# Weights converted by shifted words and fetched behind the first chunk; the two MLP products one and three steps behind attention

## The chip, the cores and the metric

The kernel runs on one NeuronCore of a Trainium2 chip. The metric is device time in microseconds, launch to end, of the compiled program. A core has a matrix engine (PE, which also has a queue of its own for loading weights into the array, PEld), VectorE (DVE), ScalarE (ACT), GpSimd (POOL) and SyncE (SP), which here only issues DMAs. Each engine takes its instructions in program order and waits on semaphores of the others.

## The reference

The input is a gated linear attention over 4 sequences of 768 tokens, 8 heads of 48, followed by an MLP with a SoLU activation and a layer norm on the resulting 3072 tokens of 384.

```python
for t in range(S):
    state = alpha[:, :, t, :, None] * state + np.einsum('bhd,bhe->bhde', k[:, :, t], v[:, :, t])
    y[:, :, t] = np.einsum('bhd,bhde->bhe', q[:, :, t], state)
...
h = x @ w_in                      # x: 3072 x 384, w_in: 384 x 1024
e = np.exp(h - h_max)
sm = e / (np.sum(e, axis=-1, keepdims=True) + 1e-09)
solu = h * sm
ln = (solu - mu) / np.sqrt(var + 1e-06) * g_ln
return (ln @ w_out).astype(np.float32)   # w_out: 1024 x 384
```

The attention inputs are float32. The weights `w_in` and `w_out` arrive as float64 and must be made float32 on the chip.

## The kernel before

The tokens are cut into 24 chunks of 128 (6 positions of each of 4 sequences; chunk n is sequence n mod 4). A main loop runs over steps n. In a step the attention of chunk n is done in matrix form, and two parts run ahead or behind it: the transposes and running products of chunk n+1 are prepared, and the MLP of chunk m = n − 3 is done, both its products in one step (`LAG = 3`, L53).

The attention of a chunk: `load` (L104) fetches alpha, q, k and v with four DMAs on SP; `prep_aq` and `prep_k` transpose them on PE (`tp`, L118) and copy them on ACT (`aT`, `qT`, `kT`, L119); `prep_scan` makes the running products with two scans on DVE (`hT` L132, `qF` L142) and a maximum over alpha (`amax`, L146); `prep_q` and `prep_k` multiply on POOL (L153, L160); `scores` (L181) makes two tiles `a` on PE, masked into `sT` on DVE (L186); `keys_back` transposes k (`tp_k`, L194); `read_out` makes `y` (L204 from the state, from a sequence's second chunk on, and L210 from the scores); `next_state` makes `kv` (L224); `x_T` transposes the result (`tp_x`, L240) into `xT`.

The MLP of a chunk: `up` makes `h` with two halves of 24 matmuls (L256; counted with the weights in two passes), then `e` = Exp(h) on ACT (L261), `u` = h·e on DVE (L262), and the square of `u` on ACT (L263). `partial` adds up eight blocks of e on POOL and of u squared on DVE (L270, L274). `down` multiplies `u` by `w_out` into `o` (L281) and adds two column sums by a matmul with ones (L286). `finish` turns the sums into the norm's scale and stores 128 rows.

The weights: before the loop three chunks are loaded; `weights` (L336) then fetches a piece of raw 64-bit words into one of 2 buffers and converts it with six DVE instructions (L349, L351, L354, L355, L356, L359), one on ACT (L350) and a multiplication on POOL (L362). It masks the mantissa's upper bits, clamps the exponent to what float32 holds, and puts sign, exponent and fraction together. `weights_in` does two of the six pieces of `w_in` in each of the steps 0 to 2; `weights_out` does the eight of `w_out` in steps 1 to 3 and scales each by the gain (L372). In step 3 `centre` (L382) makes the mean over the rows of `w_out` with eight matmuls (L386) and subtracts it with eight instructions, four on DVE and four on POOL (L391). Only then can a `down` start.

A scheduler puts the instructions of each engine in order, starting from the order of the code; it moves independent work forward. What an engine finds in its queue is fixed when the program is built. At the end the kernel checks its own assumptions (`ok`, L443 to L459); if one fails, a general path runs.

## Time and profile before

| what | value |
|---|---|
| time, median of 3 runs | 507.04 us (505.81 to 508.24) |
| profiled execution, its own time | 506.91 us |
| span of its profile | 504.0 us |
| mean granted PE clock | 0.924 |
| DMA | 30.63 MB, mean 61 GB/s |
| SP waits for conversion buffers (L344 on DVE) | 24.6 + 21.0 + 9.2 us |

A profile's page lists the busy time of each engine, the chain of work that ended last, and groups of instructions by source line. A line of a group reads: line, engine, operation, output<-inputs, shapes, count, then busy microseconds and the mean nanoseconds of one, then the idle time of the engine just before and what ended it. The granted clock is the share of full speed that PE was given; at 0.50 a matmul takes twice as long. PE's busy time is modelled, so a busy PE may be a slow one.

### The profile page before, as it was taken

How to read it: one execution, taken by the hardware profiler on the slowest of the kernel's cores; microseconds unless marked ns; L12 is line 12 of the kernel's file. 1: busy time of each engine (PE TensorE's matmuls, PEld its weight loads, DVE VectorE, ACT ScalarE, POOL GpSimd, SP SyncE). 2: the span in 40 equal slices, each digit the busy share in tenths (PEclk: the TensorE clock that was granted, in tenths of full speed). 3: DMA queues.
4: the chain of work that ended last, by engine and by line, in shares of the span. 5: the costliest groups of instructions: out<-in, count | busy, mean ns of one | idle time of the engine just before them, and what ended most of it. 6: DMA issues, size and time to landing. Idle time of an engine off the chain costs nothing.

```text
span 504.0 us, 7993 instructions
## 1 busy us (share of the span) xinstructions
PE 466.2 (93%) x3195; PEld 393.5 (78%) x3195; DVE 284.0 (56%) x555; ACT 155.9 (31%) x288; POOL 187.2 (37%) x201
## 2 busy tenths in 40 slices
PE   4898398698999999999999999999999999999993
PEld 3787276586788988898898898889889888988872
DVE  7488978975544753664565375366455535522332
ACT  4134132331323332342242333234224233423220
POOL 7233624646224423432451342343245234412232
PEclk9558555969999999999999999999999999999998
DMA  9916554400331332222123132222210100000000
GB/s 192 214 43 153 136 135 114 104 20 1 91 70 29 77 64 49 48 64 63 33 64 71 24 78 64 50 45 65 64 33 16 34 9 9 16 17 18 16 17 23
DMA packets 105663, 30.63 MB, mean 61 GB/s; under 512 B 100488, under 2 KB 103824, under 8 KB 105616
## 3 DMA queue, kind: packets, MB, share of 16 engines
q1 hardware_dynamic: 105312, 29.89, 26.1%
q8 instruction: 27, 0.44, 0.4%
q10 hardware_dynamic: 304, 0.14, 0.1%
q14 instruction: 20, 0.16, 0.1%
HBM read 25.30 MB, written 4.72 MB: 60 GB/s over the span
## 4 chain that ended last, share of the span: by engine, by line
PE 87%; DVE 8%; ACT 1%; POOL 1%; DMA 1%; issue 1%; ACTq 0%
PE o L281 25%; PE h L256 24%; PE y L210 9%; PE tp L118 7%; PE a L181 6%; PE kv L224 4%; PE y L204 3%; PE tp_k L194 2%; PE tp_x L240 2%; PE o L286 2%; PE mean L386 1%; DVE qF L142 1%; DVE expo L351 1%; DVE frac L359 1%; DVE bits L349 1%; POOL w_out L362 1%
## 5 line engine op out<-in xcount | busy, mean ns | idle before, releaser
L256 PE MATMUL h<-xT,w_in 128*128 128x128 f32 x1152 | 144.7, 281 | 3.4 <-POOL w_in L362 3.4
L256 PEld LDWEIGHTS h<-xT,w_in 128*128 128x128 f32 x1152 | 138.7, 197 | 6.3 <-POOL w_in L362 4.1
L281 PE MATMUL o<-w_out,u 128*128 128x385 f32 x384 | 129.2, 488 | 2.0 <-POOL w_out L391 2.0
L281 PEld LDWEIGHTS o<-w_out,u 128*128 128x128 f32 x384 | 71.0, 190 | 47.8 <-POOL w_out L391 3.0
L307 POOL TENSOR_TENSOR r<-sums,mhalf 128x1 f32<-128x1 f32 x24 | 13.2, 549 | 127.3 <-DVE sums L303 127.3
L210 PE MATMUL y<-vn,sT 128*128 128x48 f32 x384 | 51.5, 289 | 2.9 <-DVE sT L186 2.9
L210 PEld LDWEIGHTS y<-vn,sT 128*128 128x128 f32 x384 | 50.5, 209 | 4.5 <-DVE sT L186 3.3
L296 DVE COPY sums<-o 128x3 f32<-128x3 f32 x24 | 3.8, 160 | 89.0 <-PE o L286 89.0
L262 DVE TENSOR_TENSOR u<-h,e 128x512 f32<-128x512 f32 x48 | 32.9, 685 | 35.0 <-ACT e L261 32.3
L132 DVE TENSOR_TENSOR_SCAN hT<-aT,unit 128x516 f32<-128x516 f32 x24 | 30.3, 1263 | 38.3 <-ACT aT L119 38.3
L242 ACT COPY xT<-tp_x 128x384 f32<-128x384 f32 x24 | 11.5, 478 | 130.5 <-PE tp_x L240 130.5
L263 ACT ACTIVATE u<-u 128x512 f32<-128x512 f32 x48 | 30.2, 630 | 63.7 <-DVE u L262 55.9
L153 POOL TENSOR_TENSOR qT<-qT,qF 128x512 f32<-128x512 f32 x24 | 30.1, 1254 | 39.7 <-DVE qF L142 39.7
L261 ACT ACTIVATE e<-h 128x512 f32<-128x512 f32 x48 | 28.7, 597 | 42.5 <-PE h L256 42.5
L181 PE MATMUL a<-qT,kT 48*128 48x128 f32 x384 | 37.3, 316 | 4.8 <-POOL qT L153 4.8
L160 POOL TENSOR_TENSOR kT<-kT,hT 128x508 f32<-128x508 f32 x24 | 28.4, 1185 | 35.8 <-ACT kT L119 34.5
L270 POOL TENSOR_TENSOR part_e<-e 128x512 f32<-128x512 f32 x24 | 30.5, 1272 | 25.9 <-ACT e L261 23.8
L274 POOL TENSOR_TENSOR part_e<-part_e 128x256 f32<-128x256 f32 (+1 forms) x48 | 37.8, 787 | 3.8
L181 PEld LDWEIGHTS a<-qT,kT 48*128 48x128 f32 x384 | 30.0, 210 | 11.3 <-POOL qT L153 5.3
L172 POOL TENSOR_TENSOR state<-state,hT 128x384 f32<-128x384 f32 x20 | 16.9, 845 | 49.1 <-DVE hT L132 49.1
L142 DVE TENSOR_TENSOR_SCAN qF<-aT,seed 128x516 f32<-128x516 f32 x24 | 32.1, 1336 | 0.8
L186 DVE TENSOR_TENSOR sT<-a,mask 128x512 f32<-128x512 f32 x48 | 31.0, 680 | 0.8 <-PE a L181 0.7
(79 smaller groups left out, 572.2 us busy)
## 6 DMA issues: line engine op xcount, KB each, us to landing
vn<-in_v_dram SPq DMA_DIRECT2D x24, 192.0 KB, 2.7
an<-in_alpha_dram SPq DMA_DIRECT2D x24, 192.0 KB, 3.4
qn<-in_q_dram SPq DMA_DIRECT2D x24, 192.0 KB, 3.5
kn<-in_k_dram SPq DMA_DIRECT2D x24, 192.0 KB, 3.0
out_dram<-o_sb SPq DMA_DIRECT2D x24, 192.0 KB, 2.0
raw<-in_moe_w_in_dram SPq DMA_DIRECT2D x6, 512.0 KB, 3.8
raw<-in_moe_w_out_dram SPq DMA_DIRECT2D x8, 384.0 KB, 3.2
ident<-ident_c ACTq DMA_DIRECT2D x1, 64.0 KB, 2.3
```

What stands on the lines that cost most here:

```text
L118: nc.tensor.transpose(out=tp[:, j], in_=src[:, 2 * j : 2 * j + 2, :], identity=ident)
L132: nc.vector.tensor_tensor_scan(out=h[:, 0 : NP * SW][:, ::-1], data0=a.rearrange("p j s -> p (j s)")[:, ::-1], data1=unit.rearrange("p j s ...
L142: nc.vector.tensor_tensor_scan(out=d["qF"].rearrange("p j s -> p (j s)"), data0=a.rearrange("p j s -> p (j s)"), data1=s.rearrange("p j s ...
L181: nc.tensor.matmul(a[i][:, j], lhsT=d["kT"][heads[i], j], rhs=d["qT"][heads[i], j], start=True, stop=True)
L186: nc.vector.tensor_tensor(out=d["sT"][:, i], in0=a[i], in1=mask[:, None, :].to_broadcast([P, NP, P]), op=ALU.mult)
L210: nc.tensor.matmul(y[:, h, :], lhsT=d["sT"][:, h % 2, h // 2], rhs=d["v"][:, h], start=(c == 0 and h == 0), stop=(h == H - 1), skip_group_ ...
L256: nc.tensor.matmul(h[:, f], lhsT=w_in[:, a, (f0 + f) * P : (f0 + f + 1) * P], rhs=d["xT"][:, a], start=(a == 0), stop=(a == KC - 1),)
L262: nc.vector.tensor_tensor(out=d["u"][:, fs], in0=h, in1=d["e"][:, fs], op=ALU.mult)
L263: nc.scalar.activation(out=d["u2"][:, fs], in_=d["u"][:, fs], func=AF.Square)
L270: eng.tensor_tensor(out=t, in0=d[key][:, 0:HF], in1=d[key][:, HF:FC], op=ALU.add)
L274: eng.tensor_tensor(out=t[:, 0:w], in0=t[:, 0:w], in1=t[:, w : 2 * w], op=ALU.add)
L281: nc.tensor.matmul(o[:, 0 : DM + 1], lhsT=d["u"][:, f], rhs=w_out[:, f], start=(f == 0), stop=(f == FC - 1), skip_group_check=True,)
```

## The change

Conversion. A weight's upper word, shifted left by three and masked, with its two top bits put back, is already the float32 of the same value up to the lowest mantissa bits (`top`): the exponent's three spare bits fall out. The rest comes from the lower word times 2^-52 times the power of two in `top`. So a piece takes three DVE instructions, one on ACT, a multiplication on POOL, and an addition, on DVE for odd pieces and on POOL for even ones. Nothing clamps the exponent any more. Instead all weights are fetched once more from step 6 on, and two ACT instructions a piece (`in_range`) square the upper words, read as floats, and take Exp of −2^24 times that; their sums enter the final check.

Order. One chunk is loaded ahead of the weights instead of three; then come the fetches of all six pieces of `w_in`, then chunk 1, and so on. There are four raw buffers of their own. Three pieces of `w_in` are converted before the loop and three in step 0; `w_out` is fetched and converted in steps 0 to 2. The first product of chunk n − 1 and the second of chunk n − 3 run in step n. `down` makes its two column sums ahead of the product, from tiles of their own (`sum_e`, `sum_u`), which with `u` are kept for three chunks. `partial` does the same additions.

```diff
-    LAG = 3
+    UP, DOWN = 1, 3
...
-    xtp = pool("xtp", LAG + 1)
+    xtp = pool("xtp", UP + 2)
+    hid = pool("hid", DOWN - UP + 1)
+    rawp = pool("rawp", 4)
...
-            d["u"] = work.tile([P, FC, P], FP, name="u")
+            d["u"] = hid.tile([P, FC, P], FP, name="u")
...
             t = work.tile([P, HF, P], FP, name="part_" + key)
+            s = hid.tile([P, P], FP, name="sum_" + key)
             eng.tensor_tensor(out=t, in0=d[key][:, 0:HF], in1=d[key][:, HF:FC], op=ALU.add)
-            w = HF
+            w = HF // 2
             while w > 1:
+                eng.tensor_tensor(out=t[:, 0:w], in0=t[:, 0:w], in1=t[:, w : 2 * w], op=ALU.add)
                 w //= 2
-                eng.tensor_tensor(out=t[:, 0:w], in0=t[:, 0:w], in1=t[:, w : 2 * w], op=ALU.add)
-            d["p_" + key] = t
+            eng.tensor_tensor(out=s, in0=t[:, 0], in1=t[:, 1], op=ALU.add)
+            d["p_" + key] = s
     def down(n):
         d = st[n]
         o = ps_o.tile([P, 512], FP, tag="o", name="o")
+        for i, key in enumerate(("e", "u2")):
+            nc.tensor.matmul(
+                o[:, DM + 1 + i : DM + 2 + i], lhsT=d["p_" + key], rhs=ones[:, 0:1],
+                start=True, stop=True, skip_group_check=True,
+            )
         for f in range(FC):
             nc.tensor.matmul(
                 o[:, 0 : DM + 1], lhsT=d["u"][:, f], rhs=w_out[:, f], start=(f == 0), stop=(f == FC - 1),
                 skip_group_check=True,
-            )
-        for i, key in enumerate(("e", "u2")):
-            nc.tensor.matmul(
-                o[:, DM + 1 + i : DM + 2 + i], lhsT=d["p_" + key][:, 0], rhs=ones[:, 0:1],
-                start=False, stop=True, skip_group_check=True,
             )
...
-    for n in range(3):
-        load(n)
+    load(0)
...
-    def weights(dst, src):
-        F = dst.shape[1]
-        if src.dtype == FP:
+    float64 = moe_w_in.dtype != FP
+    IN, OUT = 512, DM
+    pieces = [(0, a, s) for s in range(0, DFF, IN) for a in range(KC)] + [(1, f, 0) for f in range(FC)]
+    def words(i):
+        kind, c, s = pieces[i]
+        rows = slice(c * P, (c + 1) * P)
+        src = moe_w_out[rows, :] if kind else moe_w_in[rows, s : s + IN]
+        dst = w_out[:, c, 0:DM] if kind else w_in[:, c, s : s + IN]
+        return src, dst
+    def fetch(i):
+        src, dst = words(i)
+        if not float64:
             nc.sync.dma_start(out=dst, in_=src)
+            return None
+        raw = rawp.tile([P, dst.shape[1], 2], U32, tag="raw", name="raw")
+        nc.sync.dma_start(out=raw.rearrange("p f w -> p (f w)"), in_=src.bitcast(U32))
+        return raw
+    raws = {}
+    def convert(i):
+        kind, c, _ = pieces[i]
+        _, dst = words(i)
+        if float64:
+            raw = raws.pop(i)
+            lo, hi = raw[:, :, 0], raw[:, :, 1]
+            F = dst.shape[1]
+            low = wtmp.tile([P, F], FP, tag="low", name="low")
+            top = wtmp.tile([P, F], U32, tag="top", name="top")
+            power = wtmp.tile([P, F], U32, tag="power", name="power")
+            nc.scalar.activation(out=low, in_=lo, func=AF.Copy, scale=2.0**-52)
+            nc.vector.tensor_scalar(
+                out=top, in0=hi, scalar1=3, scalar2=0x3FFFFFF8, op0=ALU.logical_shift_left, op1=ALU.bitwise_and
+            )
+            nc.vector.scalar_tensor_tensor(
+                out=top, in0=hi, scalar=0xC0000000, in1=top, op0=ALU.bitwise_and, op1=ALU.bitwise_or
+            )
+            nc.vector.tensor_scalar(out=power, in0=top, scalar1=0xFF800000, scalar2=None, op0=ALU.bitwise_and)
+            nc.gpsimd.tensor_tensor(out=low, in0=low, in1=power.bitcast(FP), op=ALU.mult)
+            eng = nc.vector if i % 2 else nc.gpsimd
+            eng.tensor_tensor(out=dst, in0=low, in1=top.bitcast(FP), op=ALU.add)
+        if kind:
+            nc.scalar.mul(out=dst, in_=dst, mul=g_col[:, c : c + 1])
+    far = const.tile([P, len(pieces), 2], FP, name="far")
+    def in_range(i):
+        raw = fetch(i)
+        if raw is None:
             return
-        raw = wtmp.tile([P, F, 2], U32, tag="raw", name="raw")
-        nc.sync.dma_start(out=raw.rearrange("p f w -> p (f w)"), in_=src.bitcast(U32))
-        lo, hi = raw[:, :, 0], raw[:, :, 1]
-        frac = wtmp.tile([P, F], FP, tag="frac", name="frac")
-        bits = wtmp.tile([P, F], U32, tag="bits", name="bits")
-        expo = wtmp.tile([P, F], U32, tag="expo", name="expo")
-        nc.vector.tensor_scalar(out=bits, in0=hi, scalar1=0xFFFFF, scalar2=None, op0=ALU.bitwise_and)
-        nc.scalar.activation(out=frac, in_=bits, func=AF.Copy, scale=2.0**-20, bias=1.0)
-        nc.vector.tensor_scalar(
-            out=expo, in0=hi, scalar1=1, scalar2=21, op0=ALU.logical_shift_left, op1=ALU.logical_shift_right
-        )
-        nc.vector.tensor_scalar(out=expo, in0=expo, scalar1=896.0, scalar2=1151.0, op0=ALU.max, op1=ALU.min)
-        nc.vector.tensor_scalar(out=expo, in0=expo, scalar1=896.0, scalar2=2.0**23, op0=ALU.subtract, op1=ALU.mult)
-        nc.vector.scalar_tensor_tensor(
-            out=expo, in0=hi, scalar=0x80000000, in1=expo, op0=ALU.bitwise_and, op1=ALU.bitwise_or
-        )
-        nc.vector.scalar_tensor_tensor(
-            out=frac, in0=lo, scalar=2.0**-52, in1=frac, op0=ALU.mult, op1=ALU.add
-        )
-        nc.gpsimd.tensor_tensor(out=dst, in0=expo.bitcast(FP), in1=frac, op=ALU.mult)
-    def weights_in(a):
-        for s in range(0, DFF, 512):
-            weights(w_in[:, a, s : s + 512], moe_w_in[a * P : (a + 1) * P, s : s + 512])
-    def weights_out(fs):
-        for f in fs:
-            weights(w_out[:, f, 0:DM], moe_w_out[f * P : (f + 1) * P, :])
-            nc.scalar.mul(out=w_out[:, f, 0:DM], in_=w_out[:, f, 0:DM], mul=g_col[:, f : f + 1])
+        sq = wtmp.tile([P, raw.shape[1]], FP, tag="sq", name="sq")
+        nc.scalar.activation(
+            out=sq, in_=raw[:, :, 1].bitcast(FP), func=AF.Square, accum_out=far[:, i, 0:1]
+        )
+        nc.scalar.activation(out=sq, in_=sq, func=AF.Exp, scale=-(2.0**24), accum_out=far[:, i, 1:2])
...
+    for i in range(2 * KC):
+        raws[i] = fetch(i)
+    load(1)
     prep_aq(0)
     prep_scan(0)
     prep_q(0)
     prep_k(0)
-    for n in range(N + LAG):
-        if n + 3 < N:
-            load(n + 3)
-        m = n - LAG
-        now, before, after = n < N, m >= 0, n + 1 < N
+    gains()
+    for i in range(KC):
+        convert(i)
+    nout = 2 * KC
+    for n in range(N + DOWN):
+        if n + 2 < N:
+            load(n + 2)
+        if n < DOWN:
+            mine = range(nout + n * FC // DOWN, nout + (n + 1) * FC // DOWN)
+            for i in mine:
+                raws[i] = fetch(i)
+        m, l = n - UP, n - DOWN
+        now, rise, fall, after = n < N, 0 <= m < N, l >= 0, n + 1 < N
         if after:
             prep_aq(n + 1)
-        if m > 0:
-            finish(m - 1)
+        if l > 0:
+            finish(l - 1)
         if now:
             decayed(n)
         if after:
             prep_scan(n + 1)
-        if before:
+        if rise:
             up(m, 0)
         if after:
             prep_q(n + 1)
             scores(n)
         if after:
             prep_k(n + 1)
-        if before:
+        if n == 0:
+            for i in range(KC, 2 * KC):
+                convert(i)
+        if rise:
             up(m, 1)
             partial(m)
-        if n < KC:
-            weights_in(n)
-        if n == 1:
-            gains()
-        if 1 <= n < 5 and n <= LAG:
-            per = -(-FC // LAG)
-            weights_out(range((n - 1) * per, min(FC, n * per)))
-        if n == LAG:
+        if n < DOWN:
+            for i in mine:
+                convert(i)
+        if n == DOWN:
             centre()
         if now:
             keys_back(n)
             read_out(n)
             next_state(n)
-        if before:
-            down(m)
+        if fall:
+            down(l)
         if now:
             x_T(n)
+        if 2 * DOWN <= n < 2 * DOWN + len(pieces):
+            in_range(n - 2 * DOWN)
...
+    if float64:
+        nc.vector.tensor_scalar(out=okw[:, :, 0], in0=far[:, :, 0], scalar1=2.0**34, scalar2=None, op0=ALU.is_lt)
+        nc.vector.tensor_scalar(out=okw[:, :, 1], in0=far[:, :, 1], scalar1=0.5, scalar2=None, op0=ALU.is_lt)
```

What SP finds in its queue: `vn`, `an`, `qn`, `kn` are a chunk's v, alpha, q and k, `raw` is a weight piece. The start of SP's program, before:

```order
L113 DMA vn<-in_v_dram 128x8x48
L113 DMA an_104<-in_alpha_dram 128x8x48
L113 DMA qn_96<-in_q_dram 128x8x48
L113 DMA kn_100<-in_k_dram 128x8x48
L113 DMA an_105<-in_alpha_dram 128x8x48
```

The same place now:

```order
L115 DMA vn<-in_v_dram 128x8x48
L115 DMA an_110<-in_alpha_dram 128x8x48
L115 DMA qn_102<-in_q_dram 128x8x48
L115 DMA kn_106<-in_k_dram 128x8x48
L359 DMA raw<-in_moe_w_in_dram 128x1024 x6
L115 DMA an_111<-in_alpha_dram 128x8x48
```

Chunk 1's loads, which stood right behind chunk 0's, now stand behind all six fetches of `w_in`; before, the first two of these stood behind four chunks.

DVE around the first `sT` (the masked scores of chunk 0), before:

```order
L142 SCALAR_TENSOR_TENSOR qF<-aT_108,seed_110 128x516
L132 SCALAR_TENSOR_TENSOR hT_113<-aT_109,unit 128x516
L136 COPY fend<-hT_113 128x4
L139 TENSOR_SCALAR least<-hT_113 128x4
L140 RECIPROCAL seed_111<-least 128x4
L142 SCALAR_TENSOR_TENSOR qF<-aT_109,seed_111 128x516
L146 TENSOR_REDUCE amax<-an_106 128x1
L186 TENSOR_TENSOR sT<-a_218,mask 128x512
```

And now (two more `top`, masks and `power` stand just ahead of these rows):

```order
L384 TENSOR_TENSOR w_in<-low,top 128x512
L375 TENSOR_SCALAR top<-raw 128x512
L375 TENSOR_SCALAR top<-raw 128x512
L378 SCALAR_TENSOR_TENSOR top<-raw,top 128x512 x2
L381 TENSOR_SCALAR power<-top 128x512
L148 TENSOR_REDUCE amax<-an_111 128x1
L188 TENSOR_TENSOR sT<-a_267,mask 128x512
L134 SCALAR_TENSOR_TENSOR hT_119<-aT_115,unit 128x516
```

The scans of chunk 1 went from ahead of the first `sT` to behind it, conversions of `w_in` came ahead of it, and the `amax` ahead of it is that of chunk 1.

PE ahead of the first second product (`o`, from `u` and `w_out`), before:

```order
L386 MATMUL mean<-w_out,ones 128x384
L256 MATMUL h<-xT,w_in 128x128 x14
L386 MATMUL mean<-w_out,ones 128x384
L256 MATMUL h<-xT,w_in 128x128 x9
L386 MATMUL mean<-w_out,ones 128x384
L281 MATMUL o<-w_out,u 128x385 x8
L286 MATMUL o<-ones,part_e 128x1
```

And now:

```order
L258 MATMUL h<-xT,w_in 128x128 x12
L415 MATMUL mean<-w_out,ones 128x384 x8
L196 MATMUL tp_k<-ident,kT 128x128 x4
L212 MATMUL y<-vn,sT 128x48 x8
L226 MATMUL kv<-vn,kg 128x96 x4
L285 MATMUL o<-ones,sum_e 128x1
L285 MATMUL o<-ones,sum_u_461 128x1
L290 MATMUL o<-w_out,u 128x385 x8
```

Before, the mean's matmuls were strewn among first products of chunks 0 to 2 and scores of chunks 4 and 5; now they stand together in step 3, behind the last half of chunk 2's first product, with the rest of chunk 3's attention between them and `o`.

11 lines of the change are left out of this document (7 added, 4 removed).

## The prediction

> **What bounds the kernel now.** I read the page first, then the busy time by stage, then the chain that ended last in order of time, then the groups of instructions by line.
>
> ```profile
> span 504.0 us, 7993 instructions
> PE 466.2 (93%) x3195; PEld 393.5 (78%) x3195; DVE 284.0 (56%) x555; ACT 155.9 (31%) x288; POOL 187.2 (37%) x201
> ```
>
> PE is busy for 93% of the span, but that is an average over two kernels in one: a start-up and a long even stretch. The next rows are stretches of the span: start and end, length, then busy time (and count) of PE, PE's weight loads, DVE, ACT and POOL, the granted PE clock, the DMA share and GB/s.
>
> ```profile
> 0.00:20.00 20.00, 10.72 (x64) 9.36 (x64) 13.91 (x29) 5.29 (x8) 12.28 (x23) 0.87 0.98 209
> 20.00:40.00 20.00, 20.00 (x93) 16.60 (x92) 12.92 (x23) 6.42 (x12) 5.22 (x4) 0.50 0.31 78
> 40.00:60.00 20.00, 11.06 (x76) 9.24 (x75) 18.31 (x35) 6.60 (x13) 8.89 (x7) 0.76 0.61 141
> 60.00:80.00 20.00, 17.70 (x64) 13.60 (x65) 16.00 (x32) 5.14 (x11) 4.79 (x5) 0.50 0.55 135
> 80.00:100.00 20.00, 13.78 (x95) 12.48 (x93) 18.31 (x32) 6.41 (x12) 12.20 (x9) 0.84 0.48 116
> 100.00:117.00 17.00, 14.46 (x70) 11.92 (x70) 11.25 (x20) 6.60 (x12) 7.00 (x8) 0.70 0.08 24
> 151.00:400.00 249.00, 249.00 (x1867) 214.19 (x1867) 133.60 (x264) 81.07 (x154) 90.92 (x98) 1.00 0.24 52
> ```
>
> From 151 to 400 us PE is busy all the time at full clock; nothing but fewer matmuls would help there. Before 117 us PE idles or runs at half clock, while DVE is busy for 18.31 of 20 us in the two stages that convert most weights. So the time is the start-up plus a fixed amount of PE work. The chain gives that amount (start, length, what):
>
> ```profile
> 117.28 5.45 PE o L281 x16
> ...
> 206.75 0.87 PE y L204 x8
> ...
> 210.30 5.22 PE o L281 x16
> 215.85 0.39 PE tp_x L240 x3
> ...
> 216.90 0.57 PE tp L118 x4
> 217.47 2.46 PE h L256 x22
> 219.92 1.09 PE a L181 x16
> ...
> 221.60 2.68 PE h L256 x24
> 224.28 0.44 PE tp_k L194 x4
> 224.72 0.87 PE y L204 x8
> ```
>
> One step is 224.72 − 206.75 = 17.97 us: the second product with its two column sums 215.85 − 210.30 = 5.55; the first product 48 matmuls at 2.68/24, so 5.36; the state read 0.87; the rest, the attention of a chunk, 6.2. The first second product starts at 117.28, and the last matmul of the last one is this row of the timeline:
>
> ```profile
> 495.31 0.36 PE L286 MATMUL o<-ones,part_u 128*128 128x1 f32 x2
> ```
>
> It ends at 495.67. So 378.4 us of PE work lie behind the start of the first second product, and 504.0 − 495.67 = 8.3 us of finish behind the last. **The whole question is when that product starts; call it T, now 117.3.**
>
> **What is taken off DVE.** Fourteen weight pieces (6 of 512 columns, 8 of 384) are converted. Name, shape, count, busy us and mean ns (the two L351 rows are the start-up alone, by shape):
>
> ```profile
> L349 DVE TENSOR_SCALAR bits<-raw 128x384 uint32<-128x384 uint32 (+1 forms) x14 | 9.1, 651 | 0.0
> L351 DVE TENSOR_SCALAR expo<-raw 128x384 uint32<-128x384 uint32 x8 | 7.0, 871 | 0.0
> L351 DVE TENSOR_SCALAR expo<-raw 128x512 uint32<-128x512 uint32 x6 | 2.5, 415 | 0.0
> L354 DVE TENSOR_SCALAR expo<-expo 128x384 uint32<-128x384 uint32 (+1 forms) x14 | 5.8, 413 | 0.0
> L355 DVE TENSOR_SCALAR expo<-expo 128x384 uint32<-128x384 uint32 (+1 forms) x14 | 6.5, 464 | 0.0
> L356 DVE SCALAR_TENSOR_TENSOR expo<-raw,expo 128x384 uint32<-128x384 uint32 (+1 forms) x14 | 8.9, 634 | 0.0
> L359 DVE SCALAR_TENSOR_TENSOR frac<-raw,frac 128x384 f32<-128x384 uint32 (+1 forms) x14 | 12.4, 887 | 5.0 <-ACT frac L350 5.0
> L362 POOL TENSOR_TENSOR w_out<-expo,frac 128x384 f32<-128x384 f32 x8 | 10.8, 1358 | 15.6 <-DVE expo L356 15.6
> L362 POOL TENSOR_TENSOR w_in<-expo,frac 128x512 f32<-128x512 f32 x6 | 8.8, 1466 | 8.8 <-DVE expo L356 8.8
> L391 POOL TENSOR_TENSOR w_out<-w_out,mean_sb 128x384 f32<-128x384 f32 x4 | 4.9, 1258 | 3.5 <-ACT mean_sb L388 3.5
> L391 DVE TENSOR_TENSOR w_out<-w_out,mean_sb 128x384 f32<-128x384 f32 x4 | 4.2, 1119 | 3.2 <-ACT mean_sb L388 3.2
> ```
>
> Before, DVE spends 9.1 + 9.5 + 5.8 + 6.5 + 8.9 + 12.4 = 52.2 us, 3.7 a piece. After, a piece has `top` (priced as L349, 0.65), the masking `scalar_tensor_tensor` (as L356, 0.63), `power` (mean of L354 and L355, 0.44), and for every second piece an add (as L391 on DVE, 1.12): 14 × 1.72 + 7 × 1.12 = 31.9 us, 20 less. POOL keeps one multiplication a piece (L362, 19.6 in all) and gains 7 adds (as L391 on POOL, 8.8). ACT's part stays one instruction.
>
> The L351 rows show that these prices hold waiting: the smaller shape took twice as long as the larger, in the stages where POOL is busier. The Trainium skill says, in SBUF — State Buffer, "Who interferes with whom", that such DVE instructions, and those with two SBUF inputs like the new adds, share one port pair with GpSimd, and that whichever comes second waits for a whole instruction; this trace agrees (871 against 415 ns). By that rule POOL's higher load below would lengthen each of the 31 conversion instructions of the start-up by some 0.1 us, an estimate, and the total would be 483 instead of 480.
>
> **When T comes now.** The first `sT` is the DVE instruction from which the steps run:
>
> ```profile
> 15.06 1.28 DVE L186 TENSOR_TENSOR sT<-a,mask 128x512 f32<-128x512 f32 x2
> ```
>
> In the new order four pieces' `top` and mask, three `power` and an add stand ahead of it (4 × 1.28 + 3 × 0.44 + 1.12 = 7.6 us), and the two scans of chunk 1 no longer do (about 2.5). It also stands behind the `amax` of chunk 1, whose load is now behind all of w_in on SP's queue: 0.79 MB of chunk 0 (four tiles of 128 × 8 × 48 × 4 bytes), 3.15 of w_in (384 × 1024 × 8) and 0.2 of alpha are 4.1 MB, and the first stage moved 209 GB/s × 20 us = 4.2 MB, so it lands at about 20. SP's last two w_in fetches wait for a freed buffer, as before. What queues behind that `amax` on DVE is all of step 0's rest (`sT`, so y, x and the first product) and the scan of chunk 1; on PE a transpose of chunk 1's alpha, with the same wait, stands ahead of step 0's last score matmul. With a wait for POOL's first add I take 21 (bounds 17 and 24).
>
> From there to the first centring subtraction DVE has 8 `sT`, 6 `u`, 4 pairs of scans, 3 sums of u2 and 6 `amax`: about 3.5 steps of the even stretch, at 133.60/249 × 17.97 = 9.6 us a step, 34 us. To these come 10 `top`, 10 masks, 11 `power` and 6 adds: 6.5 + 6.3 + 4.8 + 6.7 = 24.3. Together 58 us. At the 18.31/20 that DVE reached where it converted most, that takes 64 us, so **T = 85**. Its bounds: PE's own work, below (74), and DVE at the 16.00/20 of the stage 60 to 80 from 24 on (97). I take 85, since the 92% are the nearest row: same work, same engine.
>
> PE in that time: the rest of step 0 (y, kv, tp_x) 3.1, three steps of attention and first product 3 × 11.56, the mean's matmuls about as long as one second product, 5.2: 43 us. How much at half clock? These rows are stretches with PE's busy time, then its granted clock:
>
> ```profile
> 24.00:27.00 3.00, 3.00 (x15) 0.50 0.08 16
> ...
> 84.00:87.00 3.00, 3.00 (x17) 0.59 0.20 25
> 87.00:90.00 3.00, 3.00 (x26) 1.00 0.62 180
> ```
>
> Attention alone kept PE busy yet at 0.50; the first long run of first-product matmuls brought 1.00 (87 to 90). After the change such a run comes in step 1, so about 8 us of PE work stay at half clock, 8 more. With one ACT instruction for the mean (0.63, the L263 row below) and a first subtraction (1.26): 21 + 43 + 8 + 1.9 = 74. PE is not what T waits for.
>
> POOL from 21 on:
>
> ```profile
> L153 POOL TENSOR_TENSOR qT<-qT,qF 128x512 f32<-128x512 f32 x24 | 30.1, 1254 | 39.7 <-DVE qF L142 39.7
> L160 POOL TENSOR_TENSOR kT<-kT,hT 128x508 f32<-128x508 f32 x24 | 28.4, 1185 | 35.8 <-ACT kT L119 34.5 <-DVE least L139 1.3
> L270 POOL TENSOR_TENSOR part_e<-e 128x512 f32<-128x512 f32 x24 | 30.5, 1272 | 25.9 <-ACT e L261 23.8 <-PE o L286 2.2
> L274 POOL TENSOR_TENSOR part_e<-part_e 128x256 f32<-128x256 f32 (+1 forms) x48 | 37.8, 787 | 3.8
> ```
>
> 4 qT, 4 kT, 3 sums of e (1.27 + 2 × 0.79), 11 multiplications, 5 adds, a state: 5.0 + 4.7 + 8.5 + 15.3 + 6.5 + 0.8 = 41 us, below DVE's 58.
>
> **What lies behind T.** At T the old kernel had done more of chunks 4 and 5: three transposes (3 × 0.55), two groups of scores (2.2), `tp_k` (0.44); it was 6 matmuls short of chunk 2's first product (0.7), and now one `tp_x` (0.4) stands behind. So 378.4 + 4.3 − 0.7 + 0.4 = 382.3. The order within `down` and `partial` changes no count. The later fetch and range check of all weights is 6.3 MB in a stretch where DMA is 0.24 busy, and 28 ACT instructions:
>
> ```profile
> L263 ACT ACTIVATE u<-u 128x512 f32<-128x512 f32 x48 | 30.2, 630 | 63.7 <-DVE u L262 55.9 <-DVE sums L296 7.8
> ```
>
> 28 × 0.63 = 17.6 us; they stand within some three steps, where ACT idles 1 − 81.07/249 = 67%, 36 us. That hides them, save where one stands ahead of a copy that PE waits for: I take 2 us, with bounds 0 and 17.6. DVE's two more checks and a longer sum at the end are under 1 us.
>
> Sum: 85 + 382.3 + 8.3 + 2 = 477.6 of span. The profiled execution took 506.91 for its span of 504.0, so 2.9 lie around it; its median, 507.04, is the same within 0.03%. **480 us.**
>
> **The rivals.** (1) PE sets T: the conversions fit into DVE's gaps and T is 74; 74 + 382.3 + 8.3 + 2 + 2.9 = 470. For it: DVE's prices hold waiting, 415 beside 871 ns. Against: 92% busy was reached with less POOL work. (2) The same with a clock that rises in step 0: 8 us less, 462. Against it stand 20 us at 0.50 with PE busy throughout. The Trainium skill, TensorE: Matmul & The Clock Gate, "Part 1: The HAM clock gate", would have it so, since some 3.4 us of sustained work should release the clock; this trace shows otherwise for attention. (3) The clock falls back or never rises before T, as from 60 to 80: 43 us become 86, T = 21 + 86 + 1.9 = 109, 504.5: at the edge of no change. Against: a run of 24 matmuls is unbroken in the new order. (4) Slower: DVE and POOL take turns throughout. With the `top` at their bare price (0.41) that is 34 + 22 + 41 = 97 us, T = 118, 514; it costs more than the old start-up from the point where less than about 7 of POOL's 41 us lie beside DVE's work. Against: 18.31 and 12.20 of 20 us ran side by side from 80 to 100. (5) Much slower: the new range check says no, and the general path runs behind the fast one. It decides at one point: a sum of Exp at or above 0.5, or a sum of squares at or above 2^34. Read as floats, the upper words of weights near 0.05 are between 0.5 and 2, so both hold by far; but no row here shows Exp of an argument in the millions below zero. Its price is at least both products once more, 24 × (5.36 + 5.55) = 262 us: over 740.
>
> **How the numbers follow.** Forecast 0.64, own range 473 to 496; rival 1 0.22; 2 0.04; 3 0.04; 4 0.03; 5 0.03. The range is 465 (rival 1 with the first `sT` at 17) to 496 (T = 97 and a quick check, or T = 85 and the check exposed); the rest is 0.14. A measurement of this kernel tells 0.5% from no change: faster by more (below 504.5) 0.90, within 0.04 (rival 3), slower 0.06 (4 and 5).
>
> **What would show it.** Right: the first second product at 80 to 92 us, DVE about nine tenths busy from 21 to 85, clock 1.0 from the middle of step 1, steps of 17.97 behind it. PE busy throughout from 30 with T near 75 is rival 1. Clock at 0.5 past 50 is rival 3. Waits of `qn` transposes for `xT` between T and T + 60, with range-check instructions ahead on ACT, would be the check exposed. The forecast is wrong if the first `sT` comes after 24, or if the even step is no longer 17.97.

## The result, and the profile after

| | before | changed | ratio, 95% interval |
|---|---|---|---|
| median, 4 runs each | 506.43 us | 489.82 us (488.76 to 491.76) | 0.9675, 0.9629 to 0.9722 |
| profiled execution | 506.91 us | 491.76 us | |
| its span | 504.0 us | 490.0 us | |
| T, start of the first second product | 117.3 us | 89.3 us | |
| last matmul's end behind T | 378.4 us | 392.4 us | |

The kernel became 16.6 us faster; 27 had been forecast. T came 28 us earlier, as forecast within 4.3, and the work behind it grew by 14, of which 6 had been reckoned with.

The page after, the span and then busy time:

```profile
span 490.0 us, 8081 instructions
PE 461.1 (94%) x3195; PEld 389.1 (79%) x3195; DVE 264.8 (54%) x522; ACT 172.7 (35%) x344; POOL 196.1 (40%) x208
```

DVE lost 19 us of busy time and PE 5, though PE's instructions are the same 3195. The stretches, with columns as in the prediction:

```profile
20.00:40.00 20.00, 17.47 (x102) 15.77 (x103) 18.84 (x31) 7.56 (x15) 13.43 (x8) 1.00 0.80 188
40.00:60.00 20.00, 18.14 (x115) 16.75 (x114) 14.08 (x29) 8.64 (x17) 11.87 (x11) 0.74 0.55 136
60.00:80.00 20.00, 18.38 (x118) 16.75 (x117) 19.05 (x32) 10.21 (x20) 14.67 (x13) 0.74 0.61 121
100.00:117.00 17.00, 17.00 (x119) 14.17 (x119) 7.24 (x16) 14.31 (x42) 5.74 (x7) 1.00 0.85 261
151.00:400.00 249.00, 249.00 (x1841) 213.02 (x1840) 127.66 (x257) 81.25 (x152) 89.14 (x96) 1.00 0.24 51
```

From 20 us on PE is now busy for about nine tenths of the time, and from 40 to 80 DVE is busy for 33 of 40 us, with a clock of 0.74. The 1.00 of the first row doesn't hold for all of it: up to 34 us four transposes take 1.06 to 1.12 us, from there to 43 us 0.60 to 0.66. The last row is the surprise: PE is busy for all of the 249 us at full clock, as before, but got through 1841 matmuls in them where it had done 1867. The same engine, never idle in the record, does less.

The chain that ended last shows where, in one even step (start, length, what):

```profile
206.02 0.44 PE tp L120 x4
206.46 0.41 PE a L183 x2
206.87 0.58 PE tp L120 x4
207.46 2.68 PE h L258 x24
210.14 1.09 PE a L183 x14
...
218.47 0.37 PE o L285 x4
218.84 5.29 PE o L290 x16
...
224.90 0.41 PE a L183 x2
```

From one lone `a` to the next the step is 224.90 − 206.46 = 18.44 us, where it was 17.97. Before, two rows of `h` stood between the transposes of alpha and of q:

```profile
216.24 0.44 PE tp L118 x4
216.68 0.22 PE h L256 x2
216.90 0.57 PE tp L118 x4
```

The sixteen `a` rows (eight matmuls; each has two rows) then took 1.09 us together. Now two of them stand between these transposes, taking 0.41, and the other fourteen still take 1.09. Each score matmul fills 48 of the array's 128 rows, and those of even and odd heads (partitions 0 to 47 and 64 to 111) follow each other in the order. Eight of them make four pairs, and seven still need four turns: a reading of the order, not an experiment. The Trainium skill, TensorE: Matmul & The Clock Gate, "Part 3: Packing small matmuls — row/col tiling", says that matmuls on distinct row groups run side by side; 16 rows in 1.09 us, 0.07 a row, against 0.41 for a lone pair of rows, agree.

The start-up on PE (start, length from the first start to the last end, line, then in brackets the idle time ahead of the row and what ended it):

```profile
43.55 0.42 PE L212 MATMUL y<-vn,sT 128*128 128x48 f32 x2 [0.78 <-DVE sT L188]
45.06 1.22 PE L183 MATMUL a<-qT,kT 48*128 48x128 f32 x4 [1.09 <-POOL kT L162]
...
63.94 1.82 PE L212 MATMUL y<-vn,sT 128*128 128x48 f32 x14 [1.62 <-DVE sT L188]
...
72.84 4.22 PE L258 MATMUL h<-xT,w_in 128*128 128x128 f32 x24
...
77.91 2.84 PE L258 MATMUL h<-xT,w_in 128*128 128x128 f32 x24
80.59 5.33 PE L415 MATMUL mean<-w_out,ones 128*128 128x384 f32 x16
...
89.25 5.43 PE L290 MATMUL o<-w_out,u 128*128 128x385 f32 x16
```

And two rows of DVE:

```profile
22.31 0.67 DVE L188 TENSOR_TENSOR sT<-a,mask 128x512 f32<-128x512 f32 x1
...
86.49 4.25 DVE L420 TENSOR_TENSOR w_out<-w_out,mean_sb 128x384 f32<-128x384 f32 x4 [0.31 <-ACT mean_sb L417]
```

Behind the last of three waits of 0.78 to 1.62 us PE has no gap up to T, but the first 24 rows of `h` in it take 4.22 us where 24 take 2.84 at full clock. The mean's matmuls follow the last `h` at once: at the end T waited for PE.

### The profile page after: what moved, and what is told of

The parts are those of the page before. It is cut to its first block, busy times and chain, and to the rows that moved or that the text cites. A ratio compares the mean times of both kernels' runs of the same rounds, so it can differ in the third digit from the quotient of the medians.

```text
span 490.0 us, 8081 instructions
## 1 busy us (share of the span) xinstructions
PE 461.1 (94%) x3195; PEld 389.1 (79%) x3195; DVE 264.8 (54%) x522; ACT 172.7 (35%) x344; POOL 196.1 (40%) x208
## 4 chain that ended last, share of the span: by engine, by line
PE 87%; DVE 6%; POOL 3%; DMA 2%; issue 1%; ACT 0%; SPq 0%; POOLq 0%; DVEq 0%
PE o L290 26%; PE h L258 24%; PE y L212 8%; PE a L183 7%; PE tp L120 7%; PE kv L226 4%; PE y L206 4%; PE tp_k L196 2%; PE o L285 2%; POOL low L382 2%; PE tp_x L242 2%; DVE top L378 1%; DMA raw<-in_moe_w_in_dram 1%; DVE qF L144 1%; PE mean L415 1%
## 5 line engine op out<-in xcount | busy, mean ns | idle before, releaser
L258 PE MATMUL h<-xT,w_in 128*128 128x128 f32 x1152 | 138.4, 277 | 0.0
L258 PEld LDWEIGHTS h<-xT,w_in 128*128 128x128 f32 x1152 | 134.5, 194 | 0.5
L212 PE MATMUL y<-vn,sT 128*128 128x48 f32 x384 | 49.4, 283 | 2.4 <-DVE sT L188 2.4
L212 PEld LDWEIGHTS y<-vn,sT 128*128 128x128 f32 x384 | 48.2, 203 | 3.0 <-DVE sT L188 2.8
L183 PE MATMUL a<-qT,kT 48*128 48x128 f32 x384 | 44.3, 311 | 6.3 <-POOL qT L155 5.2
L183 PEld LDWEIGHTS a<-qT,kT 48*128 48x128 f32 x384 | 33.6, 200 | 14.3 <-POOL qT L155 5.3
L162 POOL TENSOR_TENSOR kT<-kT,hT 128x508 f32<-128x508 f32 x24 | 30.2, 1258 | 21.2 <-ACT kT L121 21.2
L273 POOL TENSOR_TENSOR part_e<-e 128x512 f32<-128x512 f32 x24 | 30.9, 1287 | 17.8 <-ACT e L263 17.8
L273 DVE TENSOR_TENSOR part_u<-u 128x512 f32<-128x512 f32 x24 | 18.4, 765 | 15.6 <-ACT u L265 15.6
```

The costliest lines, as they stand in the source:

```text
L162: nc.gpsimd.tensor_tensor(out=d["kT"][:, :, 0 : P - 1], in0=d["kT"][:, :, 0 : P - 1], in1=hT[n % 2][:, 0 : NP * SW].rearrange("p (j s) -> ...
L183: nc.tensor.matmul(a[i][:, j], lhsT=d["kT"][heads[i], j], rhs=d["qT"][heads[i], j], start=True, stop=True)
L212: nc.tensor.matmul(y[:, h, :], lhsT=d["sT"][:, h % 2, h // 2], rhs=d["v"][:, h], start=(c == 0 and h == 0), stop=(h == H - 1), skip_group_ ...
L258: nc.tensor.matmul(h[:, f], lhsT=w_in[:, a, (f0 + f) * P : (f0 + f + 1) * P], rhs=d["xT"][:, a], start=(a == 0), stop=(a == KC - 1),)
L273: eng.tensor_tensor(out=t, in0=d[key][:, 0:HF], in1=d[key][:, HF:FC], op=ALU.add)
```

## The experiments

Twelve runs, in four groups; each group has its own runs of the kernel before (medians 506.0 to 506.6 us).

### What lengthens the even step

**e1: the transposed result first.**

```diff
+        if now:
+            x_T(n)
         if fall:
             down(l)
-        if now:
-            x_T(n)
```

> The only edit: the transpose of attention's result (tp_x) and its copy to xT are emitted ahead of the second product instead of behind it, so that xT of chunk n-1 lies ready when step n begins and a transpose of q can follow that of alpha without a bubble. Theory A (the missing 10 us are the longer even step: two score matmuls pulled ahead as a filler, 0.41 us, with the other fourteen still taking the 1.09 of all sixteen): the step falls from 18.44 to at most 17.97, some 20 steps of it, so 489.8 becomes 480 (478 to 483). A cost of A: PE may now wait for the copy of y on ACT ahead of tp_x, up to 0.3 us a step, which would leave 486. Theory B (the range check's fetches and ACT instructions cost the 10 us) and theory C (the sums ahead of the product in the second product's group cost it): 489 to 490, step stays at 18.4.

Measured: 479.0 us (478.29 to 481.28), ratio 0.9478 (0.9446 to 0.9509). The chain of it:

```profile
159.77 5.29 PE o L290 x16
177.63 5.29 PE o L290 x16
...
218.64 0.87 PE tp L120 x8
219.51 2.68 PE h L258 x24
222.19 1.09 PE a L183 x16
```

The transposes of alpha and q stand side by side, eight in 0.87; no score stands alone; a step is 177.63 − 159.77 = 17.86. PE did not wait ahead of `tp_x`. The last second product's 5.43 us begin at 462.88, so 380.7 us lie behind T (87.64 in the same view), against a forecast of 382.3.

**e2: the first product two steps behind.**

```diff
-    UP, DOWN = 1, 3
+    UP, DOWN = 2, 3
```

> The only edit: the first product runs two steps behind attention instead of one (the second stays three behind). Theory A (the even step is longer because a first product one step behind has no xT yet when step n begins): the filler between the transposes is the first product again, scores stay whole, and the step is 17.97 as before the change, 9 us less behind the second product's start. That start itself moves later by what one step more of start-up costs, 0 to 11.6 us (an attention and a first product): 480 to 492. The step length in its trace decides, not its time. Theories B (range check) and C (order inside the second product): step stays 18.4.

Measured: 486.69 us (484.79 to 489.78), ratio 0.9615 (0.9565 to 0.9666). Its chain:

```profile
197.26 5.29 PE o L290 x16
215.27 5.29 PE o L290 x16
...
220.90 0.44 PE tp L120 x4
221.33 0.22 PE h L258 x2
221.56 0.56 PE tp L120 x4
...
224.58 1.09 PE a L183 x16
```

The bubble between the transposes is still there, but `h` of a chunk whose `xT` is long ready fills it, and the scores stay whole: 215.27 − 197.26 = 18.01 a step. Two ways of taking the split away, by moving `tp_x` or by moving the first product, both give the old step back. Theory A stands.

**e3: without the range check.**

```diff
-        if 2 * DOWN <= n < 2 * DOWN + len(pieces):
-            in_range(n - 2 * DOWN)
...
-    if float64:
+    if False:
```

> Leaves out the second fetch of all weights and the check that they are in range, with its two terms at the end. Theory A (bubble and split scores): the check lies beside PE's work, 488 to 490, at most 2 us less, step still 18.44 everywhere. Theory B (the check's 28 ACT instructions or 6.3 MB of fetches delay copies that PE waits for): 480 to 482. By the steps of the changed kernel's trace, 19.04 once and 18.22 to 18.44 otherwise while the check runs, I expect 489.0.

Measured: 489.63 us (488.21 to 491.86), ratio 0.968 (0.9643 to 0.9716): no difference from the changed kernel. Its step is 18.44 from T on, and 392.0 us lie behind its T against 392.4 in the changed kernel, so the check costs some 0.4 us. Up to T the two kernels have the same instructions in the same order on PE, DVE and POOL, and up to 88 us on ACT, yet T is 87.3 here and 89.3 there, and the 2 us are there before the check's first fetch is issued at 78.6: two executions of the same work differ by as much, and a smaller difference of T says nothing. Theory B falls. Theory C falls with e1, whose second product still begins with the two sums and whose step is shorter than the old one.

### What the two parts of the change are worth

**e4: the new conversion in the old order, and e5: the old conversion in the new order.** Each is put in place of the other conversion; the diff is e4's, over the kernel before, and e5 goes the other way:

```diff
...
-        nc.vector.tensor_scalar(out=bits, in0=hi, scalar1=0xFFFFF, scalar2=None, op0=ALU.bitwise_and)
...
+            out=top, in0=hi, scalar1=3, scalar2=0x3FFFFFF8, op0=ALU.logical_shift_left, op1=ALU.bitwise_and
...
+        turn[0] += 1
+        eng = nc.gpsimd if turn[0] % 2 else nc.vector
+        eng.tensor_tensor(out=dst, in0=low, in1=top.bitcast(FP), op=ALU.add)
```

> The kernel before, in its old order (both products three steps behind, two raw buffers, loads of three chunks first, sums behind the second product), with the new conversion alone; it leaves out the check of the weights' range, which was worth 0.2 us. DVE has 20 us less to convert. If DVE's busy time alone held the old start-up, T (start of the first second product) falls from 117 to 97 and the time to 486. If the old order holds it (raw words fetched late, PE waiting in line behind late conversions), T falls by 5 to 12 and the time is 494 to 501. I expect 496. The step behind T must stay 17.97.

> The changed kernel with the old conversion (six DVE instructions a piece, one on ACT, one on POOL); it leaves out the check of the weights' range. DVE has 20 us more to convert, POOL 9 us less. DVE theory (T = 89 is DVE's work): T rises by 20/0.92 = 22 to 111, 511 us. PE theory (T is PE's work, a third of it at half clock, and DVE has slack): T rises by 5 to 12, 495 to 502. The step must stay 18.44 in both.

Measured: e4 496.53 us (494.14 to 498.05), ratio 0.9822 (0.9792 to 0.9852); e5 499.5 us (499.27 to 499.96), 0.9873 (0.9851 to 0.9896). The conversion alone is worth 9.9 us, the order alone 6.9, together 16.8; e3, which has both and no check either, gained 16.5. The parts add up. But the order's 6.9 is a difference: its steps are 18.44 long, some 20 times 0.47 or 9.4 us, so its start-up gives about 16. Steps are 17.96 in e4 and 18.44 in e5: they go with the order. T is 100.9 in e4, between the two expectations, with 483.8 − 100.9 = 382.9 us from it to the end of the last matmul, 4.5 more than before. In e5 it is 95.6, with 0.8 us of stops inside its first product: 6 to 7 later than in the changed kernel, the PE theory's figure. But the DVE theory had put in 20 us more of DVE, and the groups of e5 show 45.0 us of conversion on DVE against the changed kernel's 34.3: 11 more. The old instructions, priced at 52.2 in the old order, were cheaper here, although POOL had no less to do (52.7 us up to 96, against 50.4 up to 117 in the kernel before); e9 and e10 below show what their price goes with.

### What sets T

**e6: chunk 1 ahead of w_in.**

```diff
+    load(1)
     for i in range(2 * KC):
         raws[i] = fetch(i)
-    load(1)
```

> The only edit: chunk 1 is loaded ahead of the six fetches of w_in instead of behind them. If the first sT (22.3 us) waits for chunk 1's load, as the wait for alpha at 20.8 says, it moves to about 18. What the whole gains tells what the second product's start (89.3) waits for: if DVE's work from the first sT on sets it, as the forecast had it, all 4 us come back and the time is 486; if PE at half clock behind late conversions sets it, or w_in's raw words, now 2 to 4 us later, delay the first product, little comes back: 488 to 491.

Measured: 495.6 us (494.04 to 495.94), ratio 0.9794 (0.9776 to 0.9812). Both figures were missed, and the first `sT` too. T is 89.6, unmoved. A row of PE and one of DVE in its trace:

```profile
21.64 0.66 PE L212 MATMUL y<-vn,sT 128*128 128x48 f32 x2 [7.64 <-DVE sT L188]
```

```profile
16.30 1.28 DVE L381 TENSOR_SCALAR power<-top 128x512 uint32<-128x512 uint32 x1
```

With chunk 1's operands there early, the scans of chunk 1 and two pieces' conversions still stood ahead of the first `sT`, which came at 20.9 instead of 22.3; `power` took 1.28 us, where 0.41 is usual for its shape in the changed kernel, and PE stood still for 7.6 us and then ran at a granted clock of 0.50 up to about 38 us. The first second product itself took 6.93 us at a lower clock. A first `sT` 1.4 us earlier brought no earlier T, though 1.4 us is less than T's scatter. Why the median is 5.8 us above the changed kernel's is not fully shown: the profiled execution, the fastest of the four, has 2.3 of them, 2.0 of which lie behind T.

**e7: PE kept busy.** Over e1:

```diff
+        for i in range({1: 10, 2: 7}.get(n, 0)):
+            nc.tensor.matmul(tp[:, 0], lhsT=ident, rhs=ident, start=True, stop=True)
```

> The kernel with tp_x first (479.0 us), and matmuls on the identity whose result is overwritten, 10 in step 1 and 7 in step 2 (0.22 us each at full clock), ahead of the transposes of k that stand before y, so that PE does not stand still where it waits for sT at 42 and 61 us. Theory P (the clock falls to half behind these waits, and the 19 us of PE work then done at half clock are on the path to T): the clock stays at 1.0 from 40 to 88, and T falls from 87.8 by 5 to 9, 470 to 474 us. Theory D (DVE's conversions set T): the clock stays up but PE then waits longer, T within 2 of 87.8, 477 to 479. If the clock falls all the same, waits of this length are not its cause.

Measured: 483.83 us (482.53 to 489.08), ratio 0.9596 (0.953 to 0.9662): 5 us slower than e1; T at 91.9, later than either theory had it. Two stretches of 5 us, and a row of PE:

```profile
55.00:60.00 5.00, 5.00 (x50) 4.88 (x50) 4.43 (x9) 1.31 (x3) 3.58 (x3) 1.00 1.09 238
60.00:65.00 5.00, 3.81 (x31) 3.19 (x30) 4.89 (x9) 3.30 (x7) 2.57 (x3) 1.00 0.45 90
```

```profile
69.69 2.02 PE L228 MATMUL kv<-vn,kg 128*128 128x96 f32 x8 [4.71 <-ACT kg L200]
```

The clock held at 1.00 up to 65 us, so PE was early, and ran into a wait of 4.7 us for a copy of the transposed k on ACT. The chain says why that copy was late:

```profile
64.75 1.18 POOL low L384
65.95 1.61 DVE w_out L386
...
68.55 0.62 ACT u L267
69.17 0.48 ACT kg L200
```

An addition on DVE waited for POOL's multiplication; ACT's scaling by the gain waited for that addition, and `u` and `kg` stood behind it in ACT's queue. Theory P in its strong form falls: a warm PE arrives earlier at a piece that isn't converted yet. Then the clock fell after all, to 0.50 from 70 to 75.

**e8: upper words alone.** Over e1; weights carry 21 bits:

```diff
...
-            nc.scalar.activation(out=low, in_=lo, func=AF.Copy, scale=2.0**-52)
...
-                out=top, in0=hi, scalar=0xC0000000, in1=top, op0=ALU.bitwise_and, op1=ALU.bitwise_or
+                out=dst.bitcast(U32), in0=hi, scalar=0xC0000000, in1=top, op0=ALU.bitwise_and, op1=ALU.bitwise_or
...
-            nc.gpsimd.tensor_tensor(out=low, in0=low, in1=power.bitcast(FP), op=ALU.mult)
...
```

> The kernel with tp_x first (479.0 us), with weights made of their upper words alone: top and its mask are left, the low word's part (an ACT instruction, power, the multiplication on POOL, the addition) is left out, so weights carry 21 bits. DVE has 14 x 0.44 + 7 x 1.12 = 14 us less, POOL 28 less. Theory D (DVE sets T): its work between the first sT and the centring falls from 58 to 46, T from 87.8 to 75, and the first sT comes 3 us earlier: 463 to 466 us. Theory P (PE's own work at half clock): T falls by the waits that vanish and the half clock behind them, 6 to 10: 469 to 473.

Measured: 460.05 us (459.51 to 466.18), ratio 0.9129 (0.9052 to 0.9206); T at 68.6, below both theories. Its stretch, then the same one of e1:

```profile
20.00:60.00 40.00, 39.80 (x335) 37.39 (x334) 34.12 (x67) 21.58 (x40) 14.92 (x15) 1.00 0.96 216
```

```profile
20.00:60.00 40.00, 35.40 (x231) 32.44 (x232) 34.47 (x62) 17.27 (x32) 27.05 (x21) 0.91 0.73 171
```

DVE is as busy in both; POOL is busy for half as long, and PE did 335 matmuls instead of 231, with no idle time to speak of. The conversion's price on DVE fell from 34.6 us to 16.6, by 18 and not by the 14 reckoned, since the two instructions that stayed got cheaper as well; T fell by 19.

**e9 and e10: all additions on POOL, all on DVE.** Over e1:

```diff
-            eng = nc.vector if i % 2 else nc.gpsimd
+            eng = nc.gpsimd
```

In e10 the new line is `eng = nc.vector`.

> The kernel with tp_x first (479.0 us; T, the start of the first second product, 87.8), with all 14 additions of the conversion on POOL: DVE has 7 x 1.1 = 7.8 us less, POOL 7 x 1.26 = 8.8 more. Theory D (DVE's own time sets T): T falls by 6 to 8, 471 to 473 us. Theory Q (the pieces pass from DVE to POOL and back, each engine in order, and the waits in line set T): DVE no longer stands behind an addition that waits for POOL, but POOL, with 50 us from the first sT on, becomes the line that others wait in: T within 3 of 87.8, 476 to 482. Theory Q is the likelier after the run with PE kept busy.

> As the kernel with tp_x first, with all 14 additions on DVE: DVE has 7.8 us more, POOL 8.8 less. Theory D: T rises by 6 to 8, 485 to 487 us. Theory Q: every piece now stops DVE for POOL's multiplication, but POOL is free sooner: T rises by 0 to 4, 479 to 483.

Measured: 481.74 us (478.99 to 482.9), ratio 0.949 (0.9435 to 0.9545), T 87.7; and 483.25 us (481.25 to 485.32), 0.955 (0.9494 to 0.9606), T 88.9 with a stop of 1.2 us in its first product. Seven additions taken off DVE or put on it moved T by about 1, less than its scatter, as theory Q had it. But the 7.8 us were never there: DVE's conversion took 30.9 us in e9 and 35.1 in e10, against 34.6 in e1. (e9 also lost time behind T, where its next second product took 7.9 us at a lower clock.) The masking instruction shows why the time did not go with the instructions. Its group (count, busy us, mean ns) in the changed kernel:

```profile
L378 DVE SCALAR_TENSOR_TENSOR top<-raw,top 128x384 uint32<-128x384 uint32 (+1 forms) x14 | 12.8, 920 | 0.1
```

In e10, where POOL has no additions:

```profile
L378 DVE SCALAR_TENSOR_TENSOR top<-raw,top 128x384 uint32<-128x384 uint32 (+1 forms) x14 | 10.9, 787 | 0.0
```

And in e12 below, where POOL has no part in the conversion:

```profile
L375 DVE SCALAR_TENSOR_TENSOR top<-raw,top 128x384 uint32<-128x384 uint32 (+1 forms) x14 | 9.0, 642 | 0.1
```

The same fourteen instructions take 0.92, 0.79 and 0.64 us each. How busy POOL is in all doesn't order them (0.89 in e9, where POOL has the most to do, and 0.98 in e1); what counts is whether an instruction of POOL is already running when the single mask begins. Two masks of one shape in the changed kernel, and the POOL instruction beside the second:

```profile
10.80 0.69 DVE L378 SCALAR_TENSOR_TENSOR top<-raw,top 128x512 uint32<-128x512 uint32 x1
...
13.94 1.45 POOL L382 TENSOR_TENSOR low<-low,power 128x512 f32<-128x512 f32 x1
14.30 1.64 DVE L378 SCALAR_TENSOR_TENSOR top<-raw,top 128x512 uint32<-128x512 uint32 x1
```

The second mask began while that instruction ran and ended 0.55 us behind its end. The traces of all fourteen kernels have 210 instructions of this kind (in the old conversion the one that puts the sign to `expo`). The 108 with no POOL instruction beside them took 0.53 to 0.56 us (384 columns) or 0.67 to 0.70 (512), and so did 36 that began ahead of the one beside them. Of the 66 that began while a POOL instruction ran, 65 ended 0.41 to 0.42 us (384) or 0.54 to 0.55 (512) behind its end, however long it still had to run; the longest took 1.67 us. In e5 thirteen of the fourteen had none beside them.

**e11: the gain folded in.** Over e1:

```diff
...
+            nc.scalar.activation(
+                out=low, in_=lo, func=AF.Copy, scale=g_low[:, c : c + 1] if kind else 2.0**-52
+            )
...
+                nc.vector.scalar_tensor_tensor(
+                    out=dst, in0=top.bitcast(FP), scalar=g_col[:, c : c + 1], in1=low, op0=ALU.mult, op1=ALU.add
+                )
...
```

> As the kernel with tp_x first, with the gain taken into the conversion of w_out: the low word is scaled by gain times 2^-52 and the upper part is multiplied by the gain in the addition (a scalar_tensor_tensor, all eight on DVE), so that ACT's eight scalings behind the additions are gone. Theory Q, with ACT as one of the lines (a copy that PE waits for stands behind a scaling that waits for a late addition, 4.7 us in the run with PE kept busy): T falls by 2 to 5, 474 to 477 us. Theory D: DVE has four additions more, 4 x 1.1, and T rises by 4: 483.

Measured: 484.07 us (483.93 to 484.33, three of four runs), ratio 0.9551 (0.9495 to 0.9608), T 90.3. ACT's scalings are gone and nothing was gained, so they are not what holds T by themselves; with four additions more on DVE, and its first product at a lower clock (8.6 us), the run can't say more. The fourth execution took 919.32 us, as long as if the general path had run too; it left no trace, and why is open. That alone would rule this version out.

**e12: the low word by a shift.** Over e1; weights are cut to 24 bits instead of rounded:

```diff
...
-            nc.scalar.activation(out=low, in_=lo, func=AF.Copy, scale=2.0**-52)
...
+            nc.vector.scalar_tensor_tensor(
+                out=dst.bitcast(U32), in0=lo, scalar=29, in1=top, op0=ALU.logical_shift_right, op1=ALU.bitwise_or
+            )
```

> The kernel with tp_x first (479.0 us), with the low word's part made of bits alone: the lower word shifted right by 29 is or-ed under top, a third DVE instruction, and ACT's scaling of the low word, power, POOL's multiplication and the addition are gone. A weight is then cut to float32's 24 bits instead of rounded to them. DVE has about as much to convert as in the kernel with tp_x first (three instructions of 0.63 to 0.9 us a piece against three and half an addition, 2 to 5 us less in all); POOL has 28 us less, ACT 8. Theory D (DVE's busy time sets T): T falls from 87.8 by 2 to 6 and the time is 473 to 477. Theory Q (the passing of a piece between ACT, DVE and POOL in order sets it): T falls nearly as far as with the upper words alone (68.8), to 70 to 76: 461 to 468 us, the fastest that keeps float32's bits. I expect 464.

Measured: 468.53 us (464.9 to 471.46, five of six runs; the sixth took 473.87), ratio 0.9252 (0.9209 to 0.9295), T 77.6: somewhat over half of what e8 gained, and between the two theories. One wait above 0.3 us is left on PE between its first `sT` and T, 1.52 us at 54; behind it the clock is 0.52 from 55 to 60.

DVE's time in the conversion, added up from the groups of each trace (`top`, mask, `power` or their old counterparts, and the additions on DVE), beside T, for the kernels in the new order:

| kernel | conversion on DVE, us | T, us |
|---|---|---|
| e8, upper words alone | 16.6 | 68.6 |
| e12, low word by a shift | 25.5 | 77.6 |
| e9, additions on POOL | 30.9 | 87.7 |
| e7, PE kept busy | 33.4 | 91.9 |
| e3, no range check | 34.0 | 87.3 |
| e2, first product two behind | 34.3 | 86.6 |
| e6, chunk 1 first | 34.3 | 89.6 |
| changed kernel | 34.3 | 89.3 |
| e1, tp_x first | 34.6 | 87.6 |
| e10, additions on DVE | 35.1 | 88.9 |
| e11, gain folded in | 36.5 | 90.3 |
| e5, old conversion | 45.0 | 95.6 |

From e8 to e5 T rises by 27.0 us for 28.4 of DVE, 0.95 a microsecond. This fits theory D once each instruction has the price that it has in its own run; with the prices of another it fails. It is not shown that DVE's time alone does it, since e8 and e12 also take the whole conversion off POOL. The nine rows between e12 and e5, whose pieces need a multiplication on POOL and an addition behind it, lie 1 to 7 us above the line from e8 to e5, and at 33 to 35 us of DVE T lies anywhere from 86.6 to 91.9: room for theory Q, for the clock and for T's scatter, which these runs can't tell apart.

Both e1 (with the changed kernel's arithmetic) and e12 beat the kernel before and the changed one.

## Why the prediction came out as it did

The sum was 85 + 382.3 + 8.3 + 2 = 477.6 of span; the profiled execution has 89.25 + 392.4 + 8.3 = 490.0, with 1.8 around it instead of 2.9. The time lies within the range of 465 to 496, and 9.8 us above the 480. Of the 12.4 us by which the profiled span passes the sum, 8.1 lie behind T (392.4 against 382.3 and the 2 for the check) and 4.3 ahead of it.

- **"So 378.4 + 4.3 − 0.7 + 0.4 = 382.3" is the step that failed** (its terms make 382.4; 392.4 was measured). It carried the old step of 17.97 into a loop in which the first product runs one step behind attention. The old order had a bubble between the transposes of alpha and q, and two rows of `h` filled it at no cost. With a lag of one, `h` isn't ready there, a score matmul fills it, and the score group costs 0.41 more. It is in the order: of the rows of a step, `a` once between two `tp`. The prediction looked at `down` and `partial` ("changes no count") and at the first steps, not at one even step. It did name the sign of it: the forecast is wrong "if the even step is no longer 17.97". By that sentence its account of the work behind T failed, though the time fell into the range. e1 and e2 show the cause, e1 with 380.7 us behind T.
- **T = 85 was right in size, by DVE's time.** The first `sT` came at 22.3 (21, bounds 17 to 24), and from it to the first centring subtraction it took 64.2 us (64). DVE was busy for 55.2 of the 64 us from 22 to 86, not the 58 at 92% that were put in, and that subtraction waited for PE's mean; that both came to 64 is in part luck. That T goes with the conversion the table above bears out. Whether the first `sT` carries on to T one for one stays open: e6 moved it by 1.4 us, less than T's scatter.
- **"PE is not what T waits for" was half wrong.** At the end PE was last. From 74, PE's sum, it came to 89: 1.3 for the later `sT`, 5 for four waits (1.7 at the first `tp_k`, and the three shown), and about 8 more at half clock than the 8 put in, since the clock fell back twice, to 0.50 from 45 to 55 and about as low from 65 to 75. That was rival 3, in part. But e7, with the clock held up to 65, was no earlier: PE then waited 4.7 us for ACT behind the conversion. Both lines end at about the same time, and only a shorter conversion brought T clearly forward.
- **DVE's conversion, 31.9 us, took 34.3.** The seven additions were cheaper (0.97 against 1.12) and the masks dearer (0.92 against 0.63). The prediction's sentence on the Trainium skill, SBUF — State Buffer, "Who interferes with whom", bears on this: a DVE instruction with two SBUF inputs shares a read port with GpSimd. The masks agree: one that begins while POOL's instruction runs ends only behind it (65 of 66, above); the 0.1 us an instruction that the prediction estimated from it was too little for them. Rival 4, engines taking turns, is this in a mild form; its 514 was far off.
- **The range check, 2 us (0 to 17.6), costs about 0.4,** hidden as argued, and the general path wasn't taken.
- **The gain of each part** was not forecast apart; T came from DVE's sum with all of it in. e4 and e5 give the conversion 9.9, and the new order's start-up about 16, of which it pays 9.4 back in its steps.

## What to carry to other kernels

Where a change shifts a stage by a step within a steady loop, write out one whole step of the new order and look for what now fills each known bubble: half a microsecond in each of 20 steps was most of the miss, and moving one line gave it back. An instruction's price belongs to the run it was read in: the same masks cost 0.64 to 0.92 us by what POOL did just then, so dividing work anew between DVE and POOL bought nothing, and taking it off both (here by bits alone) bought more than its price (18 us for the 14 reckoned in e8). Where engines wait for each other in a ring, as in this start-up, making one of them faster (PE in e7) only makes it wait at the next.

## What the runs showed of the hardware that had not been expected

The granted clock fell to 0.50 behind short waits. In the changed kernel it fell behind 0.78 + 1.09 us and behind 1.62 us of idle time, in e12 behind 1.52, and in e9 to 0.61 (105 to 110 us) behind a single wait of 0.70 us with none for 40 us ahead of it. It stayed up in e7 behind 0.74 us, and in e10 behind 1.07 us (at 67) and 1.24 us (at 91). So the length of a wait alone doesn't decide it; what does stays open. In e8, where PE waits for at most 0.29 us at a time between 20 and 440 us, it was 1.00 from 24 us on. The Trainium skill, TensorE: Matmul & The Clock Gate, "What's actually happening", has the clock gated after an idle window of about 3.4 us; these traces show falls with less idle time than that.

The prediction also had it that attention leaves the clock at half and that a run of first-product matmuls raises it. Two rows of the changed kernel, then two of e8:

```profile
34.87 0.66 PE L120 MATMUL tp<-ident,qn 128*128 128x128 f32 x4
35.37 2.84 PE L258 MATMUL h<-xT,w_in 128*128 128x128 f32 x24
```

```profile
26.65 0.60 PE L120 MATMUL tp<-ident,an 128*128 128x128 f32 x4
27.60 0.49 PE L258 MATMUL h<-xT,w_in 128*128 128x128 f32 x2
```

In both, four transposes are back from 1.1 us to 0.60 or 0.66 before the first row of `h`, in e8 within step 0, as rival 2 had it. In the kernel before, the clock stood at 0.50 from 20 to 40 us with PE busy throughout; what makes the difference stays open.

The masks had been priced at a fixed 0.63 us. As shown above, one that begins while a POOL instruction runs waits for its end (up to 1.67 us in all), and one that begins first is not lengthened (0.53 to 0.70).
